# Linear attention in chunks of 128 tokens for all heads at once, in front of two MLPs, on one Trainium2 core

## The chip, the cores and the metric

One Trainium2 chip, one of its cores. The metric is device microseconds (us) of one execution; lower is better. The engines are named as in the profile: PE (TensorE, with its weight loads as PEld), DVE (VectorE), ACT (ScalarE), POOL (GpSimd) and SP (SyncE, which issues most DMAs).

## The reference

Batch 4, 8 heads, 768 tokens, head width 48. A linear attention with a decay per channel, and two MLPs over the 3072 tokens:

```
for t in range(S):
    state = alpha[:, :, t, :, None] * state + np.einsum('bhd,bhe->bhde', k[:, :, t], v[:, :, t])
    y[:, :, t] = np.einsum('bhd,bhde->bhe', q[:, :, t], state)
x = y, heads side by side            # 3072 x 384
h = x @ w_in                         # 384 -> 2048
x = (h * sigmoid(h)) @ w_out         # 2048 -> 384
h = x @ w2_in                        # 384 -> 1024
solu = h * softmax(h)
ln = (solu - mean) / sqrt(var + 1e-06) * g_ln
out = ln @ w2_out                    # 1024 -> 384
```

## The kernel before

The tokens are cut into nine units: three of 256 tokens (batch 0) and six of 384. Attention works by chunks of 128 tokens: running products of alpha are taken with scans on DVE, q is multiplied by the product and k divided by it, and then within a chunk it is a masked product of scores with v, and between chunks a state of 48 x 48 for each head. Two heads form a pair: one on partitions 0 to 47, the other on 64 to 111.

Before, a step of attention is one pair over all the chunks of a unit (class Pair, 36 of them, four for each unit): one load `x` of q, k and alpha, two scans (`scan`, `back`), `rec`, `qmul`, `mul`; on PE the transposes of k (`tr`, line 566), the scores (`scores`, line 587), the state's contribution (`state`, lines 607 and 608), the masked scores by v (`outs`, line 638) and q by the carried state (line 645). `masked` copies one head's scores by a predicated copy on DVE, the other's by ACT and POOL. `carry` brings the state on, chunk by chunk, with tiny operations. `evac` (ACT) and `rest` (DVE) split the result into two fp32r parts in `y_all`; the fourth pair goes to `yt` and from there by DMA (`holes`) into the rows that the other three leave free, so the first MLP sees 3 x 128 full rows.

The first MLP runs in blocks: a block is 128 of the 2048 hidden features for one unit, six groups of three matmuls (three groups into `h`, lines 769 to 771; three into `x`, lines 804 to 806, two blocks later). Its weights come as packed words in 16 pieces (`d` load, `r`, `z`, `u`, `y` unpack, `c` and `p` split into two parts); a piece holds the columns or rows of two blocks. VISITS says in which order units go through the blocks.

The program has a fixed order for each engine. For the first 270 groups it is the string ORDER, one letter for a step (`a` scores, `o` outs, `p` last step of a weight piece, `g3` three groups of the MLP, and so on); a star picks another engine. After that each unit's attention is spread evenly over the MLP blocks of the unit before it (`unit_steps`). The second MLP follows for all tokens; attention is over by then.

Of the kernel before, what the change touches and what calls it, by code (L numbers as in the profile page):

```python
# [7 lines left out]
U8 = mybir.dt.uint8  # L8
# [12 lines left out]
HP = 112  # L21
KC, KF, KB = DM // 128, DFF // 128, DF2 // 128
# [4 lines left out]
RB, FB = 4, 3  # L27
# [10 lines left out]
x0 w0 K0 n0 x1 w1 i0 R0 x2 m0* q0* n1 t0 a0 F3 k0 w2 B0 x3 v0 R1 n2 d0 f0 d1 w3 d2 i1 i2 A0 R2 s0 d3* q1* r0 S0 m1  # L38
q2* t1 R3 o0 a1 k1* n3 i3 K1 f2 f1 r1 e0 B1 A1 z0 s1 m2 q3 m3 z1 t2 a2 S1* x4 o1 k2* s2 B2 A2 E0 u0 y0 e1 u1* x5 c0
S2 w4 v1 a3 d4 y1 t3 E1 r2 o2 e2 B3 k3 s3 h3 c1 p0* x6 f3 z2 A3* E2 w5 S3* o3 r3 p1 h2 r4 h1 e3 g1 u2 y2 g1 z3 u3*  # L40
z4 n4 F6 y3 E3 c2 p2* u4* c3 g1 x7 g1 p3* q4 y4 d5 r5 c4 d6 z5 d7 r6 g1 L0 g1 i4 u5 d8 R4 y5 g1 L1 g1 z6 m4 u6* f4
t4 a4 y6 p4* w6 c5 k4 g1 A4 r7 s4 p5* g2 B4 n5 R5 g1 i5 S4* L2* z7 g1 r8 m5 g1 z8 u7* o4 e4 g1 w7 c6 g1 x8 g1 d9* v2
g1 t5 q5* E4 R6 n6 p6* k5 g1 a5 A5 g1 y7 d10 f5 w8 i6 g1 R7 B5* s5 S5* L3* L4 m6 g2 c7 g3 n7 o5 e5 p7* g2 f6 t6 q6
i7 k6 E5 L5* g1 a6 m7 A6 B6 d11* f7 x9 s6 u8 S6 g1 o6 e6 y8 E6 t7 g1 q7 k7 g1 a7 B7* s7 c8 A7 h5 S7 g1 r9 o7 g1 e7
r10 E7 g1 h6 p8 z9 g1 L6 g1 r11 g1 d12* g3 u9 z10 h7 L7* u10* x10 g1 y9 g2 z11 g1 u11* g5 y10 g1 y11 d13 g1 c9 g2
c10 g2 L8 g1 p9* L9* p10* r12 z12 g1 x11 g1 u12* g1 L10* g1 d14 g2 y12 g2 L11 n8 g2 c11 g1 r13 p11* g1 c12 r14 g1
z13 d15 g1 p12* g2 L12 g1 z14 u13* g2 r15 g1 q8* g2 y13 g2 u14* L13* R8 i8 L14 c13 g6 y14 c14 m8 w9 w10 g1 z15 L15
u15* y15 g4 f8 g6 t8 p14* L16* k8* g2 n9 a8 c15 g1 i9 g4 s8 A8* g1 R9 g3 B8* m9 g1 L17* S8* g1 w11 p13* o8 t9 g1 n10
k9 L19 g1 s9 g2 R10 g1 L18 n11 g1 i10 g1 e8 g1 f9 g1 E8 g1 q9 S9* g3 m10 g1 a9 g2 L20 p15* g3 A9* B9* L21* R11 g3
L22* g2 o9 g2 e9 g1 q10 g2 L23* g1 t10 g1 E9 g1 i11 g1 m11 a10 k10 h9 s10 B10* g1 A10 S10 L24* g1 f10 g2 o10 e10 g2  # L50
t11 g3 L25 g2 E10 k11* q11 g2 s11 a11 g1 A11 S11 h10 B11* g3 o11 L26 g2 e11 E11 g2 L27 h11 g5 f11 g2 L28 W0 g1 x12
g2 L29* g3 w12 v3 x13 L30 g2 x14 n12 g3 q12* i12 g4 L31 g3 R12 g4 m12 g3 x15 w13 g1 v4 n13 L33 t12 L32 R13 k12 g1
a12 s12 g3 S12* g1 w14 q13* g3 i13 g1 A12 g1 L34* n14 g4 B12* m13 g1 o12 w15 t13 f12 L35* L36 g3 i14 g2 k13* R14 f13
g1 e12 g1 m14 q14* g1 E12 s13 L37 g4 a13 B13 A13* n15 L38* i15 x16 S13* g7 o13 g3 L39 w16 g1 n16 e13 g3 E13 a14 g1
R15 x17 g1 t14 w17 g1 B14 A14* g1 i16 g1 L40 g2 m15 k14* g1 q15* g4 s14 g2 L41* S14* o14 e14 t15 g2 R16 k15 E14 g3
f15 L42 a15 s15 m16 S15 f16 A15* B15 h14* g1 f14 g6 o15 L43* q16 g1 e15 g2 E15 g2 h15 x18 h13*
"""
RANGE = 1e28
LEAST = 1e-14
# [6 lines left out]
PAIRS = (3, 0, 1, 2)  # L66
VISITS = [(0, 0, 8), (1, 0, 8), (0, 8, 16), (1, 8, 16)] + [(u, 0, 16) for u in range(2, NU)]
# [104 lines left out]
def general(tc, qka, vt, w_in, w_out, w2_in, w2_out, g_ln, ident, mhalf, out):  # L172

    nc = tc.nc
    with (
# [4 lines left out]
        with (  # L180
# [8 lines left out]
            for p in range(H // 2):  # L189
                with tc.For_i(0, B, 1) as b:  # L190
                    x = ga.tile([HP, 3, S], F32, name="x")
                    nc.sync.dma_start(out=x, in_=qka[bass.ds(b, 1), p].rearrange("o p k s -> (o p) k s"))
# [53 lines left out]
        with (  # L246
# [4 lines left out]
            with tc.For_i(0, NT, 128) as t0:  # L251
                xt = p.tile([128, KC, 128], F32, name="xt")
                for kc in range(KC):
                    for r0, n, h0 in (
                        (0, 48, 96 * kc), (48, 16, 288 + 32 * kc), (64, 48, 96 * kc + 48), (112, 16, 304 + 32 * kc)
                    ):
                        nc.sync.dma_start(out=xt[r0 : r0 + n, kc, :], in_=yT[h0 : h0 + n, bass.ds(t0, 128)])
# [44 lines left out]
def body(tc, qka, v, vt, w_in, w_out, w2_in, w2_out, g_ln, out):  # L302
    nc = tc.nc
    with tc.tile_pool(name="const", bufs=1) as const, tc.tile_pool(name="dram", bufs=1, space=DRAM) as dram:
        ident = const.tile([128, 128], F32, name="ident")
        mask = const.tile([128, CH], I8, name="mask")
        flags = const.tile([HP, 2, NU * 4], F32, name="flags")
# [5 lines left out]
        main(tc, const, ident, mask, flags, ones, mhalf, good, x2d,  # L313
             qka, v, w_in, w_out, w2_in, w2_out, g_ln, out)

        cnt = nc.values_load(good[0:1, 0:1], min_val=0, max_val=HP)
# [4 lines left out]
def main(tc, const, ident, mask, flags, ones, mhalf, good, x2d,  # L321
# [12 lines left out]
    width = W0  # L334
    stage, att = push("stage1"), push("att0")
# [12 lines left out]
    spare = psa.tile([128, 512], F32, tag="sc", name="spare")  # L348
# [7 lines left out]
    NJ = NU * 4  # L356
    x_t, xe_t, ar_t, rb_t, ra_t = {}, {}, {}, {}, {}
    v_t, y_t, st_t, yt_t = {}, {}, {}, {}

    def upj(j):  # L360
        return j // 4, PAIRS[j % 4]

    def load_x(j, queue=nc.sync):
        if j >= NJ or j in x_t or UNITS[j // 4][2] != width:
            return
        u, p = upj(j)
        b, t0, n = UNITS[u]
        xe_t[j] = att.tile([HP, 3 * width + 1], F32, tag="x", bufs=4, name="x")
        x = xe_t[j][:, : 3 * width].rearrange("p (k s) -> p k s", k=3)
        for sl in (slice(2, 3), slice(0, 2)) if j == 0 else (slice(0, 3),):  # L370
            queue.dma_start(out=x[:, sl, :n], in_=qka[b, p, :, sl, t0 : t0 + n])
        x_t[j] = x

    def load_v(u):
        if u >= NU or UNITS[u][2] != width:
            return
        b, t0, n = UNITS[u]
        t = att.tile([128, width // CH, DM], F32, tag="v", bufs=2, name="v")
        nc.sync.dma_start(out=t[:, : n // CH, :], in_=v[b, t0 : t0 + n, :].rearrange("(c s) e -> s c e", s=CH))
        v_t[u] = t  # L380

    least = const.tile([128, 1], F32, name="least")
    nc.gpsimd.memset(least, -LEAST)
# [3 lines left out]
    d1, dr, ms = [], [], []  # L387

    def persistent():

        d1[:] = [att.tile([HP, width], F32, name=f"d1{i}") for i in range(2)]
        ms[:] = [[att.tile([128, width // CH, CH], F32, name=f"ms{i}{h}") for h in range(2)] for i in range(2)]
        dr[:] = [att.tile([HP, width], F32, name="dr")]
        for i in range(2):
            nc.gpsimd.memset(d1[i], FLOOR)
            if i == 0:
                nc.gpsimd.memset(dr[0], 0.0)
                nc.gpsimd.memset(dr[0][:, ::CH], 1.0)
            for h in range(2):
                nc.gpsimd.memset(ms[i][h], 0.0)  # L400

    persistent()
# [756 lines left out]
```

## Time and profile before

| | |
|---|---|
| median of 3 runs | 785.31 us (784.7 to 788.0) |
| the profiled execution | 786.08 us, of which 784.4 us from the first to the last instruction (the span) |
| PE, DVE, ACT, POOL busy | 96%, 54%, 46%, 19% of the span |
| instructions | 13575, of which 5290 on PE |
| mean granted PE clock | 0.993 of full speed |

Matmuls are pipelined: one is shown as busy for longer than the time after which the next can start. What a matmul costs is read from the distance between the starts of matmuls, not from its duration. An fp32 matmul of the attention stands as two instructions in the trace, an fp32r matmul of the MLPs as one.

### The profile page before, as it was taken

The page shows a single profiled execution, that of the slowest core. Times are in us where ns is not written, and L with a number is a line of the kernel's source. Part 1 is how long each engine was busy: PE and PEld are TensorE (multiplying, and loading weights), DVE is VectorE, ACT ScalarE, POOL GpSimd, SP SyncE. Part 2 cuts the span into 40 slices and gives each one's busy share as a digit, 9 for nine tenths or more (in the row PEclk, how much of TensorE's full clock was granted, in tenths as well). Part 3 has the DMA queues.
Part 4 walks back from the last instruction along what each step waited for, and adds up shares of the span by engine and source line. Part 5 has one row for each costly group of instructions (what it writes and reads, how often), then busy time and mean ns, then how long its engine had stood idle before and what let it go on. Part 6 is the DMA issues. An engine that isn't in the chain of part 4 may idle for free.

```text
span 784.4 us, 13575 instructions
## 1 busy us (share of the span) xinstructions
PE 756.9 (96%) x5290; PEld 693.8 (88%) x5291; DVE 421.6 (54%) x906; ACT 359.1 (46%) x838; POOL 150.5 (19%) x261
## 2 busy tenths in 40 slices
PE   5688999999999999999999999999999999999996
PEld 3467999999999999999999999999889999999996
DVE  6897953755443543533452442269555555555552
ACT  4766933444333433433333333377444444444442
POOL 5224413222111201211111210000221121112110
PEclk9989999999999999999999999999999999999999
DMA  8836103514122113112211100073111111111001
GB/s 268 282 123 211 55 5 96 146 32 116 34 57 62 58 38 89 57 32 76 76 33 32 62 6 6 7 272 101 61 51 41 41 41 41 47 45 50 31 21 36
DMA packets 35657, 57.59 MB, mean 73 GB/s; under 512 B 3040, under 2 KB 30496, under 8 KB 35584
## 3 DMA queue, kind: packets, MB, share of 16 engines
q1 hardware_dynamic: 34880, 53.30, 21.9%
q10 hardware_dynamic: 704, 3.34, 1.2%
q8 instruction: 43, 0.70, 0.4%
q14 instruction: 30, 0.25, 0.1%
HBM read 44.83 MB, written 9.44 MB: 69 GB/s over the span
## 4 chain that ended last, share of the span: by engine, by line
PE 90%; DMA 1%; ACT 1%; POOL 1%; DVE 1%; issue 0%; SPq 0%; POOLq 0%; ACTq 0%
PE x L804 9%; PE h L769 9%; PE x L805 8%; PE x L806 8%; PE h L770 8%; PE h L771 8%; PE h L1020 4%; PE o L1068 4%; PE h L1021 4%; PE h L1022 4%; PE o L1066 4%; PE o L1067 4%; PE sc L587 3%; PE y L638 3%; PE tp L1045 3%; PE y L645 3%
## 5 line engine op out<-in xcount | busy, mean ns | idle before, releaser
L775 ACT ACTIVATE g<-h 128x384 fp32r<-128x384 f32 (+1 forms) x144 | 65.8, 457 | 196.8 <-PE h L771 196.4
L769 PE MATMUL h<-y_all,w1i 128*128 128x384 f32 (+1 forms) x432 | 144.2, 334 | 4.9 <-DMA y_all<-yt 4.9
L804 PE MATMUL x<-g,w1o 128*128 128x384 f32 (+1 forms) x432 | 143.0, 331 | 0.0
L805 PE MATMUL x<-g,w1o 128*128 128x384 f32 (+1 forms) x432 | 138.3, 320 | 1.3 <-POOL g L779 1.3
L770 PE MATMUL h<-y_all,w1i 128*128 128x384 f32 (+1 forms) x432 | 138.4, 320 | 0.0
L771 PE MATMUL h<-y_all,w1i 128*128 128x384 f32 (+1 forms) x432 | 138.3, 320 | 0.0
L806 PE MATMUL x<-g,w1o 128*128 128x384 f32 (+1 forms) x432 | 138.1, 320 | 0.0
L769 PEld LDWEIGHTS h<-y_all,w1i 128*128 128x128 f32 x432 | 82.8, 192 | 10.4 <-issue 8.4
L779 DVE TENSOR_TENSOR g<-g,g 128x384 fp32r<-128x384 f32 (+1 forms) x125 | 67.8, 545 | 39.3 <-ACT g L776 39.2
L804 PEld LDWEIGHTS x<-g,w1o 128*128 128x128 f32 x432 | 82.4, 191 | 4.9 <-issue 2.8
L805 PEld LDWEIGHTS x<-g,w1o 128*128 128x128 f32 x432 | 82.5, 191 | 1.7 <-POOL g L779 1.7
L770 PEld LDWEIGHTS h<-y_all,w1i 128*128 128x128 f32 x432 | 83.0, 192 | 0.1
L771 PEld LDWEIGHTS h<-y_all,w1i 128*128 128x128 f32 x432 | 82.9, 192 | 0.0
L806 PEld LDWEIGHTS x<-g,w1o 128*128 128x128 f32 x432 | 82.4, 191 | 0.0
L596 POOL TENSOR_SCALAR_AFFINE_SELECT ms<-ms 128x384 f32<-128x384 f32 (+1 forms) x39 | 22.4, 579 | 267.4 <-ACT ms L595 267.3
L1066 PE MATMUL o<-w2o,ct 128*128 128x384 f32 x192 | 66.5, 346 | 0.0
L776 ACT ACTIVATE g<-h 128x384 f32<-128x384 f32 (+1 forms) x144 | 65.2, 453 | 0.7 <-POOL g L779 0.7
L1068 PE MATMUL o<-w2o,ct 128*128 128x384 f32 x192 | 64.7, 337 | 0.0
L1067 PE MATMUL o<-w2o,ct 128*128 128x384 f32 x192 | 64.6, 337 | 0.0
L666 DVE TENSOR_TENSOR y_all<-y,y_all 112x384 fp32r<-112x384 f32 (+2 forms) x28 | 14.2, 508 | 91.2 <-ACT y_all L661 91.1
L132 DVE TENSOR_REDUCE nm<-h 128x1 f32<-128x1024 f32 x24 | 29.4, 1224 | 57.7 <-PE h L1022 57.7
L1020 PE MATMUL h<-w2i,x 128*128 128x512 f32 x144 | 56.8, 394 | 0.0
(121 smaller groups left out, 1356.3 us busy)
## 6 DMA issues: line engine op xcount, KB each, us to landing
x<-in_qka_dram SPq DMA_DIRECT2D x24, 504.0 KB, 4.4
raw<-in_w_in_dram SPq DMA_DIRECT2D x10, 768.0 KB, 6.9
raw<-in_w_out_dram SPq DMA_DIRECT2D x8, 768.0 KB, 6.2
x2f<-x2d SPq DMA_DIRECT2D x24, 192.0 KB, 2.8
out_dram<-ob SPq DMA_DIRECT2D x24, 192.0 KB, 1.9
x<-in_qka_dram SPq DMA_DIRECT2D x11, 336.0 KB, 4.8
v<-in_v_dram SPq DMA_DIRECT2D x6, 576.0 KB, 5.3
x2d<-x_all SPq DMA_DIRECT2D x5, 576.0 KB, 2.7
```

Of the source, the lines that this page charges most:

```text
L769: nc.tensor.matmul(h, w1i[:, 0, kc, fs], Y[:, kc, 0, :n], start=(kc == 0), stop=False)
L770: nc.tensor.matmul(h, w1i[:, 0, kc, fs], Y[:, kc, 1, :n], start=False, stop=False)
L771: nc.tensor.matmul(h, w1i[:, 1, kc, fs], Y[:, kc, 0, :n], start=False, stop=(kc == KC - 1))
L775: nc.scalar.activation(out=g[:, 0, :n], in_=h, func=AF.Silu)
L779: eng.tensor_tensor(out=g[:, 1, :n], in0=g32[:, :n], in1=g[:, 0, :n].bitcast(F32), op=ALU.subtract)
L804: nc.tensor.matmul(x, w1o[:, 0, f, msl], g[:, 0, :n], start=first, stop=False)
L805: nc.tensor.matmul(x, w1o[:, 0, f, msl], g[:, 1, :n], start=False, stop=False)
L806: nc.tensor.matmul(x, w1o[:, 1, f, msl], g[:, 0, :n], start=False, stop=last)
L1020: nc.tensor.matmul(h[:, sl], x[:, 0, kc, :], self.w2i[:, 0, kc, sl], start=(kc == 0), stop=False)
L1066: nc.tensor.matmul(o, ct[:, 0, kb, :], self.w2o[:, 0, kb, :], start=(kb == 0), stop=False)
L1067: nc.tensor.matmul(o, ct[:, 0, kb, :], self.w2o[:, 1, kb, :], start=False, stop=False)
L1068: nc.tensor.matmul(o, ct[:, 1, kb, :], self.w2o[:, 0, kb, :], start=False, stop=(kb == KB - 1))
```

## The change

A step of attention is now one chunk of 128 tokens with all four pairs side by side (class Chunk, 24 of them, two or three for each unit). The same scans, products, transposes, scores and sums are made, four pairs of 128 columns in one instruction on DVE, ACT and POOL where there were two or three chunks of one pair. The products of k and q take their input from a layout in which a chunk is contiguous; the reciprocal of a chunk's last product now goes into the start of the backward scan, so that `mul` is one plain product; the two flags of a pair become one. `carry` is one or two operations for all heads. Both masked copies run on DVE in `unit_steps`; the ORDER string chooses for the first units.

In `outs` the even pairs go to PSUM bank sA and the odd ones to sB, and an odd pair's heads are swapped: head 0 on input partitions 0 to 47 is written to output partitions 64 to 111, and head 1 the other way round. The scores use the same two banks. The fourth pair's rows are again moved by `holes`, now all six DMAs at the end of a unit. Rows of `w_in` are permuted to fit.

Pools: three buffers instead of four for loaded `x` and for raw weights, one d1 tile instead of two. VISITS gives the first two units blocks 0 to 4 and 0 to 8, then 4 to 16 and 8 to 16. ORDER is written anew; it holds no filling matmuls (`F`). At the end the last store is issued by ACT, and the flag of the check is read into the engines' registers ahead of it.

```diff
-RB, FB = 4, 3
+XB, RB, FB = 3, 3, 3
...
-VISITS = [(0, 0, 8), (1, 0, 8), (0, 8, 16), (1, 8, 16)] + [(u, 0, 16) for u in range(2, NU)]
+VISITS = [(0, 0, 4), (1, 0, 8), (0, 4, 16), (1, 8, 16)] + [(u, 0, 16) for u in range(2, NU)]
...
+            nc.vector.tensor_tensor_scan(
+                out=rb_t[c][:, ::-1], data0=xe_t[c][:, o + NS : o : -1], data1=dr, initial=0.0,
+                op0=ALU.mult, op1=ALU.max,
+            )
...
+        def mul(eng=nc.vector):
+            x = x_t[c]
+            eng.tensor_tensor(out=x[:, 1, :], in0=x[:, 1, :], in1=rb_t[c], op=ALU.mult)
...
+            for p in range(NP):
+                sl = slice(p * CH, p * CH + CH)
+                for i, (lo, hi) in enumerate(HD):
+                    nc.tensor.matmul(self.sc[i][:, p, :], x[lo:hi, 1, sl], x[lo:hi, 0, sl], start=True, stop=True)
...
+            if not self.first:
+                nc.vector.tensor_tensor(out=st[:, 1], in0=z, in1=st_t[self.c - 1][:, 0], op=ALU.add)
+                z = st[:, 1]
+            nc.vector.tensor_tensor(out=st[:, 0], in0=z, in1=ends, op=ALU.mult)
...
+            self.y = y = [self.bank(t, o) for t, o in (("sA", "x1"), ("sB", "x2"))]
+            where = []
+            for p in range(NP):
+                sl = slice(p // 2 * CH, p // 2 * CH + CH)
+                for i, (lo, hi) in enumerate(HD):
+                    where.append((p, i, lo, hi, y[p % 2], 64 * (i ^ (p % 2)), sl))
+            for p, i, lo, hi, bank, r, sl in where:
+                w = D if r else 64
+                e0 = (2 * p + i) * D
+                nc.tensor.matmul(
+                    bank[r : r + w, sl], vv[:, e0 : e0 + w], ms[i][:, p, :],
+                    start=p < 2, stop=self.first, skip_group_check=True,
+                )
+            if not self.first:
+                st = st_t[self.c - 1]
+                for p, i, lo, hi, bank, r, sl in where:
                     nc.tensor.matmul(
+                        bank[r : r + D, sl], st[lo:hi, 0, p, :], x[lo:hi, 0, p * CH : p * CH + CH],
+                        start=False, stop=True, skip_group_check=True,
                     )
...
             r += [
+                step(0, [lambda c=c: load_x(c + XB - 1), lambda c=c: load_v(c + 1), Q.tr, Q.keep]),
+                step(1, [Q.scores, lambda Q=Q: Q.masked(0, True), lambda Q=Q: Q.masked(1)]),
+                step(2, [Q.state, Q.outs, lambda Q=Q: Q.evac(1), lambda Q=Q: Q.evac(0), Q.carry]),
+                step(3, [lambda Q=Q: Q.rest(1), lambda Q=Q: Q.rest(0)]),
             ]
+        return r + [lambda: [holes(u, kc) for kc in range(KC)]]
...
+            if i == n - 1:
+                queue = nc.scalar
+                self.cnt = nc.values_load(self.good[0:1, 0:1], min_val=0, max_val=HP)
+            queue.dma_start(out=self.out[t : t + 128, :], in_=ob)
```

PE, one visit of `outs` from the fourth unit on. Before, one pair over three chunks, the two heads in turn (ms is the masked scores, v the values, x holds q, st the carried state; the size is partitions by columns of the output):

```order
L638 MATMUL y<-ms_1598,v 64x128
L638 MATMUL y<-ms_1599,v 48x128
L638 MATMUL y<-ms_1598,v 64x128
L638 MATMUL y<-ms_1599,v 48x128
L638 MATMUL y<-ms_1598,v 64x128
L638 MATMUL y<-ms_1599,v 48x128
L645 MATMUL y<-x,st 48x128 x4
```

And now, one chunk with four pairs:

```order
L608 MATMUL sA<-ms_108,v 64x128
L608 MATMUL sA<-ms_109,v 48x128
L608 MATMUL sB<-ms_108,v 48x128
L608 MATMUL sB<-ms_109,v 64x128
L608 MATMUL sA<-ms_108,v 64x128
L608 MATMUL sA<-ms_109,v 48x128
L608 MATMUL sB<-ms_108,v 48x128
L608 MATMUL sB<-ms_109,v 64x128
L615 MATMUL sA<-x,st 48x128 x2
L615 MATMUL sB<-x,st 48x128 x2
L615 MATMUL sA<-x,st 48x128 x2
L615 MATMUL sB<-x,st 48x128 x2
```

A unit of 384 tokens now has three such visits where it had four; each holds four pairs. Output partitions run 0, 64, 64, 0 in the L608 rows where they ran 0, 64, 0, 64, and pairs of rows alternate between two banks.

DVE, around the last weight piece (the last `p`, line 458 before, line 450 now; `g` is the low part of an MLP block, `f` a weight piece being unpacked). Before:

```order
L482 SCALAR_TENSOR_TENSOR ar<-x,d_107 112x256
L500 RECIPROCAL ra<-ar 112x2
L666 TENSOR_TENSOR yt<-y,yt 112x256
L623 TENSOR_TENSOR st<-tz,st 112x48
L509 SCALAR_TENSOR_TENSOR x<-x,ra,rb 112x128 x2
L779 TENSOR_TENSOR g<-g_1253,g 128x256
L458 TENSOR_TENSOR w1o<-f,w1o 128x768
```

Now:

```order
L642 TENSOR_TENSOR yt<-sB,yt 112x128
L642 TENSOR_TENSOR y_all<-sB,y_all 112x128
L642 TENSOR_TENSOR y_all<-sA,y_all 112x2x128
L91 SCALAR_TENSOR_TENSOR f<-f 128x768
L100 TENSOR_SCALAR f<-f 128x768
L744 TENSOR_TENSOR g<-g_1157,g 128x256
L106 SCALAR_TENSOR_TENSOR f<-raw,f 128x768
L744 TENSOR_TENSOR g<-g_1213,g 128x256
L450 TENSOR_TENSOR w1o<-f,w1o 128x768
```

Ahead of the last piece there stood the first result of the third unit (its `yt`, the first of its four pairs); now all six chunks of the first three units are finished there. In the order of the whole program, 127 groups of the MLP stood ahead of the last `p` before, and 136 stand there now.

## Rows read from the trace of the kernel before

**Rows 1.** The page: busy us, share of the span, instructions by engine.

```profile
PE 756.9 (96%) x5290; PEld 693.8 (88%) x5291; DVE 421.6 (54%) x906; ACT 359.1 (46%) x838; POOL 150.5 (19%) x261
```

**Rows 2.** Timeline, PE, the start (start us, us, idle and its releaser in brackets).

```profile
30.66 0.55 PE L769 MATMUL h<-y_all,w1i 128*128 128x256 f32 x1 [3.19 <-DMA y_all<-yt]
...
37.03 0.28 PE L770 MATMUL h<-y_all,w1i 128*128 128x256 f32 x1
37.15 0.28 PE L771 MATMUL h<-y_all,w1i 128*128 128x256 f32 x1
41.82 0.58 PE L566 MATMUL tz<-ident,x 112*128 112x112 f32 x2 [4.39 <-DVE x L509]
```

**Rows 3.** Windows up to the last weight piece: all engines, then lines 769, 804, 638.

```profile
0.00:107.00 107.00, 86.05 (x670) 72.11 (x672) 86.52 (x164) 71.29 (x174) 39.23 (x75) 0.95 0.52 172
...
0.00:107.00 107.00, 21.27 (x66) 13.82 (x66) 0.95 0.52 172
...
0.00:107.00 107.00, 18.14 (x58) 12.01 (x59) 0.95 0.52 172
...
0.00:107.00 107.00, 8.57 (x72) 5.51 (x72) 0.95 0.52 172
```

**Rows 4.** Groups by line and shape, DVE, whole span (busy us, mean ns).

```profile
L482 DVE TENSOR_TENSOR_SCAN ar<-x,d 112x384 f32<-112x384 f32 x24 | 24.4, 1015 | 1.3 <-DMA v<-in_v_dram 1.3
L593 DVE COPY_PREDICATED ms<-mask,sc 128x384 f32<-128x384 uint8 x24 | 14.2, 592 | 35.2 <-PE sc L587 35.2
L482 DVE TENSOR_TENSOR_SCAN ar<-x,d 112x256 f32<-112x256 f32 x12 | 9.1, 758 | 5.0 <-POOL x L470 5.0
L593 DVE COPY_PREDICATED ms<-mask,sc 128x256 f32<-128x256 uint8 x9 | 3.8, 439 | 4.0 <-PE sc L587 4.0
```

**Rows 5.** Timeline, DVE: the last weight piece.

```profile
106.96 0.95 DVE L458 TENSOR_TENSOR w1o<-f,w1o 128x768 fp32r<-128x768 f32 x1
```

**Rows 6.** Timeline, PE, 200 to 220 us: attention's visits among the MLP's matmuls.

```profile
206.61 0.34 PE L806 MATMUL x<-g,w1o 128*128 128x384 f32 x1
206.79 0.36 PE L566 MATMUL tz<-ident,x 112*128 112x112 f32 x2
...
207.17 0.34 PE L805 MATMUL x<-g,w1o 128*128 128x384 f32 x1
...
209.43 0.34 PE L771 MATMUL h<-y_all,w1i 128*128 128x384 f32 x1
209.70 0.26 PE L607 MATMUL tz<-v,kt 128*64 128x48 f32 x1
...
209.92 0.88 PE L638 MATMUL y<-ms,v 128*48 128x128 f32 x12
210.73 0.86 PE L645 MATMUL y<-x,st 48*48 48x128 f32 x12
...
211.80 0.34 PE L805 MATMUL x<-g,w1o 128*128 128x384 f32 x1
211.98 0.34 PE L806 MATMUL x<-g,w1o 128*128 128x384 f32 x1
...
214.58 0.34 PE L771 MATMUL h<-y_all,w1i 128*128 128x384 f32 x1
214.85 0.94 PE L587 MATMUL sc<-x 48*128 48x128 f32 x12
...
216.00 0.34 PE L805 MATMUL x<-g,w1o 128*128 128x384 f32 x1
```

**Rows 7.** Timeline, PE: the same line earlier, with eight instructions.

```profile
56.09 0.65 PE L638 MATMUL y<-ms,v 128*64 128x128 f32 x8
```

**Rows 8.** Timeline, PE's weight loads and matmuls of one visit.

```profile
236.99 0.63 PEld L638 LDWEIGHTS y<-ms,v 128*64 128x64 f32 x12 [0.25 <-issue]
236.99 0.87 PE L638 MATMUL y<-ms,v 128*64 128x128 f32 x12
```

**Rows 9.** The page: DMA issues, KB each, us to landing.

```profile
raw<-in_w_in_dram SPq DMA_DIRECT2D x10, 768.0 KB, 6.9
```

More of the change, by code (lines that the diff above doesn't have):

```diff
@@ L532, in prep_pieces, with prepare @@
+        if c <= LEDC:
             return dict(n=scan, q=qmul, R=back, i=rec, m=mul, f=flag)
-        return [first, back, rec, mul, flag]
-    queue = [(j, f) for j in range(4 * LED + 1, NJ) for f in prep_pieces(j)]
-    def prepare(j, part=1.0):
-        if j not in x_t:
+        return [first, second, mul, flag]
+    queue = [(c, f) for c in range(LEDC + 1, NC) for f in prep_pieces(c)]
+    def prepare(c, part=1.0):
+        if c not in x_t:
             return
-        left = sum(1 for jj, _ in queue if jj <= j)
+        left = sum(1 for cc, _ in queue if cc <= c)
@@ L601, in state @@
         def state(self):
-            kt, tz, vv, p = self.kt, self.tz, v_t[self.u], self.p
-            z = tz[:HP, 3 * HP : 3 * HP + 3 * D].rearrange("p (c e) -> p c e", e=D)
-            h0 = 2 * p * D
-            for c in range(self.nz):
-                k0 = c * HP
-                nc.tensor.matmul(z[0:64, c, :], kt[:, k0 : k0 + 64], vv[:, c, h0 : h0 + D], start=True, stop=True)
+            if self.last:
+                return
+            kt, vv = self.kt, v_t[self.c]
+            self.z = z = self.tz[:HP, : NP * D].rearrange("p (c e) -> p c e", e=D)
@@ new lines, in evac, with rest, holes @@
+        def evac(self, k):
+            for y, hi, _ in self.places(k):
+                nc.scalar.copy(hi, y)
+        def rest(self, k):
+            for y, hi, lo in self.places(k):
+                nc.vector.tensor_tensor(out=lo, in0=y, in1=hi.bitcast(F32), op=ALU.subtract)
+    def holes(u, kc, queue=nc.sync):
+        n = UNITS[u][2]
+        for r in range(2):
+            j = 32 * kc + 16 * r
+            src = j if j < D else 64 + j - D
+            queue.dma_start(
+                out=y_t[u][48 + 64 * r : 64 + 64 * r, kc, :, :n].bitcast(F32),
+                in_=yt_t[u][src : src + 16, :, :n].bitcast(F32),
+            )
@@ L687, in unit_steps, with step @@
     def unit_steps(u):
         r = []
-        pairs = [Pair(j) for j in range(4 * u, 4 * u + 4)]
-        def close(P):
-            return [P.outs, P.evac, P.rest] + ([P.holes] if P.p < 3 else [])
-        for k, P in enumerate(pairs):
-            j = P.j
-            def step(i, fns, j=j):
+        for c in range(NC):
+            if UNIT_OF[c] != u:
+                continue
+            Q = Chunk(c)
+            def step(i, fns, c=c):
                 def run():
                     if i == 0:
-                        prepare(j)
+                        prepare(c)
@@ L744, in step @@
         if letter in "xvw":
-            return dict(x=lambda j: load_x(j, queue), v=load_v, w=floors)[letter](i)
-        if letter in "FKW":
-            return dict(F=lambda: fill(i), K=halves if i else constants, W=widen)[letter]()
-        P = first[i]
+            return dict(x=lambda c: load_x(c, queue), v=load_v, w=floors)[letter](i)
+        if letter in "FK":
+            return dict(F=lambda: fill(i), K=halves if i else constants)[letter]()
+        if letter == "h":
+            return holes(i // KC, i % KC, queue)
+        Q = first[i]
         return dict(
-            t=P.tr, k=lambda: P.keep(other), a=P.scores, A=lambda: P.masked(0, other),
-            B=lambda: P.masked(1, other), s=P.state, S=lambda: P.carry(other),
-            o=P.outs, e=P.evac, E=P.rest, h=lambda: P.holes(queue),
+            t=Q.tr, k=lambda: Q.keep(other), a=Q.scores, A=lambda: Q.masked(0, other),
+            B=lambda: Q.masked(1, other), s=Q.state, S=Q.carry, o=Q.outs,
+            e=lambda: Q.evac(0), E=lambda: Q.rest(0), j=lambda: Q.evac(1), J=lambda: Q.rest(1),
         )[letter]()
@@ L808, in fn @@
                     xs = xs_of(u)
-                    if blocks[gi][1] >= KF // 2 and (u, 0, KF) not in VISITS:
+                    if again[gi]:
                         nc.vector.tensor_tensor(out=xs[:, m, :], in0=x, in1=xs[:, m, :], op=ALU.add)
@@ L822, in main @@
     visits = VISITS
-    blocks = []
+    blocks, again = [], []
     start = {}
```

389 lines of the change are left out of this document (150 added, 239 removed).

## The prediction

> **What bounds the kernel now.** I read the page first: PE is busy for 96% of the span and no other engine for more than 54% [rows 1], so what counts is PE's own work, and the places where PE has none. The timeline of PE at the start is next: the first MLP matmul begins at 30.66 us, and after 37.15 us PE stops for 4.39 us behind DVE [rows 2]. The windows tell why: up to the last weight piece, which DVE starts at 106.96 us [rows 5], DVE is busy for 86.5 of 107 us, ACT for 71.3, and the clock averages 0.95 [rows 3]. So there are two stretches. To about 108 us DVE sets the pace: it unpacks weights and prepares attention while PE waits or fills in. Behind that PE sets it. The second is read from the timeline in the middle, where MLP matmuls of 384 columns start 0.17 to 0.18 us apart and attention visits stand between them [rows 6]. What a visit costs is the time from the last matmul ahead of it to the second behind it, less two matmuls (0.35 us), since that second one is the first to run at its usual distance.
>
> **The change part by part, behind 108 us.** The counts of matmuls stay: 192 scores, 192 masked products, 160 with the state, 160 state sums, 80 transposes. What changes is how many share a visit. From [rows 6]: 12 score instructions 216.00 - 214.58 - 0.35 = 1.07 us; two transposes 207.17 - 206.61 - 0.35 = 0.21; a visit of 8 state, 12 masked and 12 carried instructions 211.80 - 209.43 - 0.35 = 2.02. Four more instructions of 128 columns cost 0.22 (x12 takes 0.87 or 0.88, x8 takes 0.65 [rows 6, 7]), so two run at a time at 0.11 a pair. Eight state instructions take 209.92 - 209.70 = 0.22.
>
> Before, units 3 to 8 (three batches of two units): a pair of a batch's first unit has 12 state, 12 masked and 8 carried instructions and three transposes, 0.32 + 1.07 + (2.02 + 0.11 - 0.22) = 3.30 us; one of its second unit 0.21 + 1.07 + 2.02 = 3.30. Eight pairs make 26.4 us a batch. After, a chunk has 16 of each: scores 1.07 + 0.22 = 1.29; four transposes 0.42 (between 0.21, if it is all overhead, and twice that; I take the upper); a full outs visit 2.02 + 0.22 + 0.22 + 0.22 = 2.68. The first chunk of a batch has nothing carried (12 instructions, 0.66, less): 2.02 + 0.22 + 0.22 - 0.66 = 1.80; the last has no state sums and no transposes: 2.02 - 0.22 + 0.44 = 2.24. A batch: 6 x 1.29 + 5 x 0.42 + 4 x 2.68 + 1.80 + 2.24 = 24.6 us. That is 1.8 less, **5.4 us** for three batches, from entering and leaving the visits' array modes three times a unit instead of four. Below zero it cannot go, since no instruction is added.
>
> The swap comes on top. Before, the carried products alternate between two 64 x 64 quarters of the array (input rows 0 to 47 to output 0 to 47, and 64 to 111 to 64 to 111), and 12 of them take six times 0.11. Now an even and an odd pair together use all four quarters, with the odd pair in another bank. No row shows four quarters at work. Bounds: 0.88 us for 16 if still two run at a time, 0.44 if four do. I take four: the state visit shows that instructions can start every 0.22 / 8 = 0.028 us [rows 6], and four in 0.11 need just that. Five chunks a batch carry: 5 x 0.44 = 2.2, **6.6 us** for three batches.
>
> Here the Trainium skill speaks against it. [rows 8] show weight loads for the next masked products going on (0.63 us, all 12) inside the 0.87 us of matmuls that use the same 128 input rows. TensorE: Matmul & The Clock Gate (Part 3, "What overlaps and what doesn't") says that a weight load overlaps matmuls in flight only when the row group differs; TensorEngine Tiling (Restrictions and Gotchas, Gotcha 1) that different row tiles cannot be in one PSUM bank at once. By the first, two quarters on the same input rows would take turns and the 6.6 us would not come; the trace does not bear it out for two column halves. By the second, the old pair of quarters, which shares bank y, would take turns too, and 0.11 us for two shows that it does not.
>
> The masked products now go to outputs 0, 64, 64, 0. Each half gets as many as before; I cost the order at nothing (at most half again of 0.88 us: 0.44 for each of 24 chunks, 10 us).
>
> DVE behind 108 us: a chunk asks for about 6.5 us, three in a unit's 61 us, so only bursts matter. The longest is two masked copies (592 ns at 384 columns and 439 at 256 [rows 4], so 0.745 at 512), the reciprocal (0.2) and a backward scan (1.15): 2.8 us, and then the 0.56 us for the low part of a block. That part is needed 18 matmuls of 0.17 us (3.1 us) behind where it is queued; a burst that hits it squarely costs 0.3 us. With the six DMAs of holes now all at a unit's end I allow **1 us** in all (0 to 4).
>
> **Up to 108 us.** Priced by row means, with 512 columns carried on from 256 and 384 (scan 758, 1015, so 1272 ns [rows 4]), DVE's list up to its last weight piece sums to 96.4 us before and 95.5 after: weights 47.5 and 45.1, MLP low parts and copies 6.7 and 8.1, attention 42.2 and 42.3. So I leave the last piece at 107.9 us. What differs is what PE has done by then. Before: (66 + 58) instructions of lines 769 and 804 are 124 groups, and 72 / 8 = nine pairs have their y [rows 3]; a tenth has its scores and transposes. After, 136 groups and all six chunks, which are twelve pairs, stand ahead of that piece in the order. Twelve groups of three matmuls 0.12 apart [rows 2] are 4.3 us; three pairs of 256 tokens at 0.85 + 0.21 + (2.02 - 0.44) = 2.64 are 7.9, less 1.05 for the tenth's start: **11.2 us**. PE can have done it: from 30.66 us, 136 x 0.36 = 49 and four chunks of 4.4 = 18 lead to 97 us, ten under the piece. Bounds: DVE idles for 20 of the 107 us, and half of that may go with the fewer small steps (21 us gained); six more us of waits for the second unit leave 5.
>
> The store by ACT and the early flag: I take nothing.
>
> **The sum**, against the profiled execution: 784.4 - 11.2 - 5.4 - 6.6 + 1.0 = 762.2 us of span; that execution took 1.7 us more than its span, so **763.9 us**. It was 786.1, 0.8 above the median.
>
> **The rivals.** *Two quarters at a time*: the 6.6 us stay away, 770.5. *Nothing won at the start*: the second unit's MLP blocks are due after four blocks of the first instead of eight. If its two chunks are late (four DVE-bound chunks at some 6 us of DVE work each, with three pieces between), PE idles there, the clock falls, and the 11.2 us are given back: 775.1. For it: PE already waited for DVE in that place. Against: DVE's list has these chunks at 42 us of its own work. *Slower: the raw weights' ring.* Three buffers instead of four. Before, 16 pieces in about 103 us are 25.7 us a turn of a buffer, of which the load takes 6.9 [rows 9] and four unpacking steps at 0.95 another 3.8; the rest is waiting. If a turn keeps its 25.7 us, three buffers need 137 us, the last piece lands some 33 us late and the time is about 797 (763.9 + 33). It decides from a turn of about 24 us on, where the whole gain is gone. Against: the waiting is for DVE and ACT, which the new order serves piece by piece. *No change*: two at a time and nothing won at the start, 781.7.
>
> **How the numbers follow.** Forecast as summed 0.42, two at a time 0.24, nothing won at the start 0.18 (some of it with two at a time), no change 0.08, slower 0.08. The range 750 to 777 runs from the sum with 10 us more at the start and some cover for the 1 us, to nothing won at the start with 2 us more of bursts. Changes within 0.5% (3.9 us) can't be told from none here: faster 0.86, same 0.07, slower 0.07.
>
> **What would show it.** Line 615 x16 in 0.6 us (four quarters) or about 1.0 (two); an outs visit among 384-column matmuls at 2.2 or 2.7 us; scores at 1.3; the last piece of line 450 at 100 to 108 us, with some 136 instructions of lines 734 and 769 and 96 of line 608 ahead of it; no idle in front of PE's lines 735 and 770 behind 110 us. I am wrong if PE waits for line 450 or for `y_all` for over 10 us past 45 us, if masked products take over 1.3 us for 16, or if bursts on DVE stop PE each chunk.

## The result, and the profile after

The changed kernel takes 762.98 us (median of 4 runs, 761.04 to 764.04), the kernel before 785.98 beside it (784.7 to 788.0): a ratio of 0.970, with a 95% interval from 0.967 to 0.973. The profiled execution took 764.04 us, with a span of 762.3: 22.0 us less than the span of before. The forecast was 763.9.

The page of the changed kernel, busy time by engine, beside [rows 1]:

```profile
PE 726.5 (95%) x5282; PEld 682.2 (89%) x5282; DVE 404.4 (53%) x728; ACT 342.0 (45%) x730; POOL 138.4 (18%) x196
```

PE has eight instructions fewer; DVE has 178 fewer and is busy for 17 us less. PE is still the bound.

Timeline of PE in the changed kernel: the start with five of its six longest gaps, block 8 (the ninth block), and the only gap of over 1 us from 60 to 108 us, beside [rows 2]:

```profile
12.41 0.58 PE L557 MATMUL sA<-x 48*128 48x128 f32 x1 [12.41 <-DVE x L485]
...
20.82 0.58 PE L557 MATMUL sA<-x 48*128 48x128 f32 x1 [1.95 <-DVE x L485]
...
33.82 0.58 PE L557 MATMUL sA<-x 48*128 48x128 f32 x1 [4.16 <-POOL x L485]
...
36.52 0.56 PE L734 MATMUL h<-y_all,w1i 128*128 128x256 f32 x1
...
54.91 0.34 PE L557 MATMUL sA<-x 48*128 48x128 f32 x1 [4.68 <-DVE x L485]
...
59.23 0.55 PE L734 MATMUL h<-y_all,w1i 128*128 128x256 f32 x1 [1.68 <-DMA y_all<-yt]
...
69.24 0.28 PE L734 MATMUL h<-y_all,w1i 128*128 128x256 f32 x1
...
91.72 0.39 PE L770 MATMUL x<-g,w1o 128*128 128x256 f32 x1 [1.59 <-DVE g L744]
```

The first MLP matmul comes six us later than before (36.52 against 30.66), yet PE has caught up by block 8 (69.24 us; before, 70.37). Windows of the changed kernel (busy us and instructions of PE, PEld, DVE, ACT, POOL, then granted clock, DMA share, GB/s): all engines to 107 us, lines 734, 769 and 608 alone, beside [rows 3], then two stretches:

```profile
0.00:107.00 107.00, 77.96 (x753) 72.11 (x754) 86.75 (x127) 68.66 (x137) 34.43 (x50) 0.97 0.61 186
...
0.00:107.00 107.00, 20.22 (x67) 13.74 (x68) 0.97 0.61 186
...
0.00:107.00 107.00, 17.61 (x60) 11.75 (x60) 0.97 0.61 186
...
0.00:107.00 107.00, 8.79 (x96) 7.11 (x96) 0.97 0.61 186
...
31.00:61.00 30.00, 20.66 (x218) 18.58 (x219) 29.44 (x45) 18.16 (x36) 8.35 (x11) 0.91 0.72 216
...
75.00:108.00 33.00, 31.41 (x314) 29.98 (x313) 29.20 (x43) 24.62 (x54) 11.07 (x8) 1.00 0.39 130
```

All six chunks have their masked products (96) by 107 us, but only 67 + 60 = 127 MLP instructions of these two lines stand beside them, three more than before. From 75 to 108 us PE lacks 1.59 us, and that is the one wait at 91.72. The last weight piece, beside [rows 5], is three and a half us later than before:

```profile
110.47 0.96 DVE L450 TENSOR_TENSOR w1o<-f,w1o 128x768 fp32r<-128x768 f32 x1 [0.57 <-ACT w1o L447]
```

The visits are as forecast. Timeline of PE in the changed kernel, a full visit for the outputs, beside [rows 6] (the fp32 instructions stand one by one here):

```profile
256.25 0.34 PE L736 MATMUL h<-y_all,w1i 128*128 128x384 f32 x1
256.52 0.26 PE L579 MATMUL sT<-v,kt 128*64 128x48 f32 x1
...
257.16 0.47 PE L608 MATMUL sB<-ms,v 128*48 128x128 f32 x4
257.38 0.47 PE L608 MATMUL sA<-ms,v 128*48 128x128 f32 x4
257.60 0.47 PE L608 MATMUL sB<-ms,v 128*48 128x128 f32 x4
258.00 0.31 PE L615 MATMUL sA<-x,st 48*48 48x128 f32 x2
258.01 0.31 PE L615 MATMUL sB<-x,st 48*48 48x128 f32 x2
258.15 0.28 PE L615 MATMUL sA<-x,st 48*48 48x128 f32 x2
258.16 0.28 PE L615 MATMUL sB<-x,st 48*48 48x128 f32 x2
258.26 0.28 PE L615 MATMUL sA<-x,st 48*48 48x128 f32 x2
258.27 0.28 PE L615 MATMUL sB<-x,st 48*48 48x128 f32 x2
...
258.59 0.45 PE L769 MATMUL x<-g,w1o 128*128 128x384 f32 x1
258.87 0.34 PE L770 MATMUL x<-g,w1o 128*128 128x384 f32 x1
```

By the measure of the prediction the visit costs 258.87 - 256.25 - 0.35 = 2.27 us (2.24 forecast with four quarters, 2.68 with two). Line 615 starts four instructions every 0.11 us; the masked products, all on 128 input rows, two (four every 0.22). Over the stretch from 190 to 470 us the medians are 1.30 for scores, 0.40 for transposes, 2.27, and 1.68 and 1.81 for the first and last chunk: 6 x 1.30 + 5 x 0.40 + 4 x 2.27 + 1.68 + 1.81 = 22.4 us a batch, and the forecast was 24.6 - 2.2 = 22.4.

### The profile page after: what moved, and what is told of

It is laid out like the page before. It is cut to its first block, busy times and chain, and to the rows that moved or that the text cites. A ratio compares the mean times of both kernels' runs of the same rounds, so it can differ in the third digit from the quotient of the medians.

```text
span 762.3 us, 13151 instructions
## 1 busy us (share of the span) xinstructions
PE 726.5 (95%) x5282; PEld 682.2 (89%) x5282; DVE 404.4 (53%) x728; ACT 342.0 (45%) x730; POOL 138.4 (18%) x196
## 4 chain that ended last, share of the span: by engine, by line
PE 91%; DMA 3%; DVE 3%; ACT 2%; issue 1%; SPq 0%; DVEq 0%; ACTq 0%
PE h L734 9%; PE x L769 9%; PE x L770 9%; PE x L771 9%; PE h L736 9%; PE h L735 8%; PE o L1030 4%; PE h L984 4%; PE o L1031 4%; PE h L985 4%; PE h L986 4%; PE o L1032 4%; PE sA L557 3%; PE tp L1009 3%; DMA raw<-in_w_out_dram 2%; PE sA L608 1%
## 5 line engine op out<-in xcount | busy, mean ns | idle before, releaser
L740 ACT ACTIVATE g<-h 128x384 fp32r<-128x384 f32 (+1 forms) x144 | 65.9, 458 | 165.7 <-PE h L736 165.6
L769 PE MATMUL x<-g,w1o 128*128 128x384 f32 (+1 forms) x432 | 139.0, 322 | 0.0
L770 PE MATMUL x<-g,w1o 128*128 128x384 f32 (+1 forms) x432 | 137.3, 318 | 1.6 <-DVE g L744 1.6
L771 PE MATMUL x<-g,w1o 128*128 128x384 f32 (+1 forms) x432 | 137.2, 317 | 0.0
L744 DVE TENSOR_TENSOR g<-g,g 128x384 fp32r<-128x384 f32 (+1 forms) x126 | 71.2, 572 | 85.3 <-ACT g L741 84.8
L984 PE MATMUL h<-w2i,x 128*128 128x512 f32 x144 | 57.0, 396 | 0.0
L985 PE MATMUL h<-w2i,x 128*128 128x512 f32 x144 | 56.9, 395 | 0.0
L986 PE MATMUL h<-w2i,x 128*128 128x512 f32 x144 | 56.9, 395 | 0.0
```

Source lines behind the costliest of these rows:

```text
L769: nc.tensor.matmul(x, w1o[:, 0, f, msl], g[:, 0, :n], start=first, stop=False)
L770: nc.tensor.matmul(x, w1o[:, 0, f, msl], g[:, 1, :n], start=False, stop=False)
L771: nc.tensor.matmul(x, w1o[:, 1, f, msl], g[:, 0, :n], start=False, stop=last)
L984: nc.tensor.matmul(h[:, sl], x[:, 0, kc, :], self.w2i[:, 0, kc, sl], start=(kc == 0), stop=False)
L985: nc.tensor.matmul(h[:, sl], x[:, 0, kc, :], self.w2i[:, 1, kc, sl], start=False, stop=False)
L986: nc.tensor.matmul(h[:, sl], x[:, 1, kc, :], self.w2i[:, 0, kc, sl], start=False, stop=(kc == KC - 1))
```

## The experiments

Each was timed with the kernel before on the same chip. The interval is that of the ratio; the span is that of the profiled execution. Block 8 is the start of the ninth block's first MLP matmul in the profile (69.2 us in the changed kernel).

| kernel | median us (lowest to highest) | ratio [95%] | span | block 8 |
|---|---|---|---|---|
| no swap | 769.25 (766.5 to 770.98) | 0.978 [0.975, 0.982] | 768.6 | 69.0 |
| state apart | 769.32 (767.25 to 769.77) | 0.979 [0.977, 0.982] | 765.5 | 68.5 |
| m2 on DVE | 762.91 (761.21 to 763.65) | 0.971 [0.968, 0.973] | 761.3 | 68.6 |
| two chunks first | 762.24 (761.05 to 766.3) | 0.972 [0.968, 0.975] | 759.3 | 66.4 |
| three signs left out | 761.02 (760.47 to 763.48) | 0.968 [0.965, 0.971] | 759.0 | 65.9 |
| transposes with scores | 763.78 (762.54 to 765.39) | 0.971 [0.968, 0.973] | 762.9 | 69.9 |
| last store by SP | 763.13 (one run) | | 761.4 | 68.8 |
| two chunks first, store by SP | 761.74 (760.09 to 764.39) | 0.970 [0.969, 0.972] | 762.6 | 69.6 |
| the same, two signs elsewhere | 762.61 (761.17 to 764.69) | 0.972 [0.970, 0.974] | 761.1 | 68.4 |
| the same, two low parts elsewhere | 762.53 (761.77 to 762.97) | 0.972 [0.970, 0.973] | 760.8 | 67.9 |
| the changed kernel again | 763.27 (762.43 to 764.53) | 0.973 [0.972, 0.974] | 762.2 | 69.2 |
| fifteen signs left out | 760.89 (758.56 to 761.72) | 0.968 [0.965, 0.970] | 760.0 | 69.1 |

**Is it the four quarters?** The swap alone is taken back, with the row maps that belong to it.

```diff
-    swap = kc % 2
+    swap = 0
...
-                    where.append((p, i, lo, hi, y[p % 2], 64 * (i ^ (p % 2)), sl))
+                    where.append((p, i, lo, hi, y[p % 2], 64 * i, sl))
```

> The changed kernel with the odd pairs not swapped: head 0 of every pair goes to output partitions 0 to 47, head 1 to 64 to 111, in the same two banks, and the rows of the first weight matrix are permuted to fit; all else stays. Theory (the swap lets four quarters of the array work at once): the 16 carried products of a chunk take 0.87 us in place of about 0.44, an outs visit 2.7 us in place of 2.27, and with 20 such chunks, 13 of them behind block 48, the time is 6 to 9 us more than the changed kernel's 763, so 769 to 772. Rival (the products gained by sharing a visit, and the quarters take turns anyway): no change, 763. Second rival (the order 0, 64, 64, 0 of the masked products holds them up): some of the loss is given back in line 608, and the time is below 769.

The carried products of one visit in its timeline of PE:

```profile
260.26 0.42 PE L615 MATMUL sA<-x,st 48*48 48x128 f32 x4
260.51 0.39 PE L615 MATMUL sB<-x,st 48*48 48x128 f32 x4
260.73 0.39 PE L615 MATMUL sA<-x,st 48*48 48x128 f32 x4
260.95 0.39 PE L615 MATMUL sB<-x,st 48*48 48x128 f32 x4
```

Now four take 0.22 us, two at a time. All other visits keep their price, and the full one costs 2.70 instead of 2.27: 0.42 more, where 0.44 was reckoned. From unit 3's first block to the last matmul of the first MLP 13 visits make 5.5, and that stretch is 5.3 us longer (365.9 against 360.6); the time rose by 6.3. So the swap is worth what the forecast said, and two banks without it are worth nothing. Whether the swap within one bank would do as much was not tried.

**Is a visit's entry what the rest of the gain is?** The state sums go into a visit of their own.

```diff
-                step(2, [Q.state, Q.outs, lambda Q=Q: Q.evac(1), lambda Q=Q: Q.evac(0), Q.carry]),
+                Q.state,
+                step(2, [Q.outs, lambda Q=Q: Q.evac(1), lambda Q=Q: Q.evac(0), Q.carry]),
```

> The changed kernel with the state sums of a chunk in a step of their own from the fifth unit on, so that each of 12 chunks there has four visits of PE in place of three; no instruction is added. Theory (entering and leaving a visit costs PE time, which is what four pairs in a visit save): each apart visit costs 0.33 us, the difference in the trace of before between the two apart (0.68 + 1.57) and the two together (1.92); 12 x 0.33 = 4 us, 767. Rival (visits cost nothing, the gain came from the swap and the start alone): 763.

The end of a state visit in its timeline of PE (line 735 is the MLP's):

```profile
256.16 0.28 PE L579 MATMUL sT<-v,kt 128*64 128x48 f32 x2
256.37 0.44 PE L735 MATMUL h<-y_all,w1i 128*128 128x384 f32 x1
256.65 0.34 PE L736 MATMUL h<-y_all,w1i 128*128 128x384 f32 x1
```

The two visits cost 0.79 + 1.81 us against 2.27 together: 0.33 more, as forecast, and 12 of them 3.9. The same stretch is 4.2 us longer. The median rose by 6.3, more than that; the profiled execution, at 767.25, was its shortest, so the other 2 us are in no profile and stay open.

**Does every visit have this price?** The opposite: the transposes join the scores' visit.

```diff
-                step(0, [lambda c=c: load_x(c + XB - 1), lambda c=c: load_v(c + 1), Q.tr, Q.keep]),
-                step(1, [Q.scores, lambda Q=Q: Q.masked(0, True), lambda Q=Q: Q.masked(1)]),
+                step(0, [lambda c=c: load_x(c + XB - 1), lambda c=c: load_v(c + 1)]),
+                step(1, [Q.tr, Q.scores, Q.keep, lambda Q=Q: Q.masked(0, True), lambda Q=Q: Q.masked(1)]),
```

> The changed kernel with the four transposes of a chunk in the visit of its scores instead of a visit of their own; only the chunks of units 4 to 8, 12 with transposes. If every visit costs a fixed price of about 0.35 to 0.4 us for entering and leaving, as the prediction reckoned it for three visits instead of four, 12 fewer give 4.2 to 4.8 us: 758 to 759 us, and the merged visit takes 1.30 + 0.05. If the price is that of going over to quarters of the array, which the scores pay anyway, and transposes on all rows pay only the 0.09 us by which the second matmul behind them is late, 12 give 1.1 us: 762, and the merged visit takes 1.6 us.

```profile
250.99 0.34 PE L736 MATMUL h<-y_all,w1i 128*128 128x384 f32 x1
251.17 0.55 PE L538 MATMUL sT<-ident,x 112*128 112x112 f32 x4
251.64 0.37 PE L557 MATMUL sA<-x 48*128 48x128 f32 x1
...
252.74 0.45 PE L734 MATMUL h<-y_all,w1i 128*128 128x384 f32 x1
253.02 0.34 PE L735 MATMUL h<-y_all,w1i 128*128 128x384 f32 x1
```

This is the merged visit in its timeline of PE: 253.02 - 250.99 - 0.35 = 1.68 us, against 0.40 + 1.30 apart. Nothing is won (0.02 a chunk), and both theories were too high. Behind an MLP matmul the transposes start at its usual distance of 0.18, so entering costs them nothing. What is saved, 0.09 at leaving them and 0.10 at the scores' own entry, comes back between the two: the scores begin 0.47 us behind the transposes, where in the changed kernel the MLP begins 0.32 behind. This fits a price for going over to parts of the array, and not one for each visit; these two regroupings are all that was tried.

**Does DVE's list pace the start?** First, the long product of chunk 2, in front of which PE stands for 4.16 us, is moved from POOL to DVE (`m2*` becomes `m2` in ORDER).

> The changed kernel with the product of k of the third chunk on DVE in place of POOL, for whose result PE waits 4.2 us just ahead of the first MLP block. Theory (in the first 60 us DVE's list sets when the second unit is ready, and PE's waits there only change their place): the first MLP block starts 1 to 4 us earlier, PE waits as much longer ahead of the fourth block, and the time is within 1 us of 763. Rival (each wait of PE at the start counts in full): 759.

No change, and block 8 at 68.6: PE's wait ahead of these scores stays where it was (4.99 us at 32.79), now for DVE. Then the order of DVE's list: the first two chunks' scans and products stand ahead of the first weight piece.

```diff
-x0 w0 d0 v0 K1 r0 n0 x1 x2* i0 R0 v1 q0* z0 d1 m0 u0* K0 y0 a0 t0 w1 n1 f0 B0 w2 i1 k0 s0 r1 A0* o0 q1* d2 c0 r2 j0
+x0 w0 x1 d0 v0 K1 n0 v1 x2 d1 i0 R0 q0* m0 K0 a0 t0 w1 n1 i1 q1* R1 A0* m1 r0 z0 u0* y0 f0 B0 w2 k0 s0 r1 o0 d2 c0 r2 j0
```

> The changed kernel with another order of the first 30 us alone: the load of the second chunk goes ahead of the first weight piece, and the preparation of both chunks stands on DVE ahead of the first unpacking step, which there waits 3.1 us for its load with the product of the first chunk behind it. Theory (the start lost time because attention's first chain stood behind a weight load; PE has no idle time behind 61 us, so what the start loses is lost for good): the first scores at 8 to 9 us in place of 12.4, the first MLP block 3 to 6 us earlier than 36.5, and the time 2 to 5 us less, 758 to 761. Rival (weights are what the start waits for): the first MLP block comes earlier, the following ones do not, and the time is the same or longer.

Its profile was 3.0 us shorter, its median only 0.7, well within the spread of its runs. Then work is left out: the step that gives the sign back to the weights.

```diff
-... q0* z0 d1 m0 ... t1 z1 d3 f1 ... c2 z3 n3 f2 ...
+... q0* d1 m0 ... t1 d3 f1 ... c2 n3 f2 ...
```

> The changed kernel without the step that gives the sign back (line 91 on DVE) to weight pieces 0, 1 and 3, so these weights are wrong; the other pieces keep it. That takes three DVE instructions of about 0.95 us from the first 55 us, 2.9 us in all. If DVE's list sets the pace there, the first MLP matmul of block 4 comes 2 to 3 us earlier than 59.2 us, that of block 8 2 to 3 us earlier than 69.2, and the run ends at 760 to 761 us. If transfers set the pace (the DMA engines are 82% busy up to 31 us), block 4 moves by less than 1 us and the time stays at 763.

This looked like proof: block 8 at 65.9, 3.3 us earlier, and 761.02. But "two chunks first" had looked as good in one profile, so it was run again with the store, beside two ways to take 1.9 us from DVE without leaving anything out (`z1`, `z3` starred; `p2`, `p3` unstarred) and the changed kernel itself.

> The changed kernel with two edits that looked better in a trace alone: the preparation of the first two chunks ahead of the first weight piece (the span was 3.0 us shorter with it), and the last store on SP's queue (0.46 us shorter tail). If both are real, they add: 763.0 - 2.6 (block 8 came at 66.4 instead of about 69.0 us) - 0.5 = 759.9 us. Rival: a start that is earlier in one profile is within what the start varies by from run to run (block 8 came at 68.5 to 69.9 us in six kernels that start alike), and the median stays at 762 to 763.

> The kernel with both edits, and the signs of weight pieces 1 and 3 given back by ACT and POOL (0.9 us and 2.1 us) instead of DVE (0.95 us). If what counts at the start is the sum of DVE's list, as the run without three signs says (3.1 us earlier for 2.9 us less), block 8 comes 1.9 us earlier than in the kernel with both edits: at 64.5 us, and the time falls by 1.9 us. Rival: the piece is late by the longer way over two engines, and DVE waits for it in its next step of the same piece: no gain, or a loss of 1 to 2 us.

> The kernel with both edits, and the low parts of weight pieces 2 and 3 on POOL (2.4 us each) instead of DVE (0.95 us). Nothing on DVE waits for a low part, only the matmuls of blocks 2 and 3. If the sum of DVE's list counts, block 8 comes 1.9 us earlier, at 64.5 us. Rival: POOL's other work behind it, the products of line 485 and the half of the masked copies, comes 2.4 us later and holds up the scores: no gain or a loss.

> The changed kernel once more, beside the three others on one chip: 763 us, with block 8 at 68.5 to 69.9 us. If the three others gain what was said, it stands 3 to 5 us behind them.

The 66.4 us of block 8 did not come back: the same start gave 69.6, and with 1.9 us less on DVE 68.4 and 67.9, not 64.5. On this chip all four medians lie within 1.6 us, with intervals that overlap; none is a faster kernel that could be vouched for. The last run takes the sign from fifteen of the sixteen pieces.

> The changed kernel without the step that gives the sign back (line 91 on DVE) to fifteen of the sixteen weight pieces of the first MLP, so these weights are wrong. It takes seven DVE instructions (6.5 us) from the first 61 us and eight more behind them. If DVE's list paces the first 61 us, block 8 comes 5 to 6.5 us earlier than the 68.5 to 69.9 us of the kernels that start alike, at 62.5 to 64 us, and since PE is busy without a break from about 61 us on, the eight later ones give nothing more: 757 to 758 us. If DVE paced PE up to 108 us, as the prediction said, all fifteen would count: 749 us. Rival: transfers or the steps on ACT and POOL pace the start, what the run without three signs gained was the spread of the starts, and the time stays at 761 to 763.

The theory falls: some 14 us of DVE's work are gone, and 2 us were won. The start of block 8 in its timeline of PE, and windows of this kernel, the same two stretches as above:

```profile
69.15 0.28 PE L734 MATMUL h<-y_all,w1i 128*128 128x256 f32 x1
```

```profile
31.00:61.00 30.00, 22.17 (x221) 20.04 (x222) 24.74 (x40) 18.08 (x36) 8.76 (x10) 0.74 0.76 221
75.00:108.00 33.00, 33.00 (x329) 31.76 (x328) 24.32 (x40) 25.83 (x56) 7.41 (x8) 1.00 0.46 142
```

DVE has 4.7 us less to do between 31 and 61 us, and block 8 comes at 69.1 all the same. (PE, granted 0.74 of its clock there instead of 0.91, is busy for 1.5 us more, so that much of a gain may be hidden; 5 to 6.5 us were expected.) The 2 us that were won lie behind: block 16 starts at 88.7 us (88.8 with the signs), block 20 at 98.6 (100.5), because the one wait at 91.72 is gone and PE is busy for 33.00 of 33. Why three signs left out gave more at block 8 than fifteen is open. In that profile the second weight piece landed earliest of all (below), but only 0.75 us ahead of the next, which is too little for 3 us.

What holds the first MLP matmul is seen on the queues. ACT in the changed kernel, then DVE (timelines):

```profile
9.88 0.89 ACT L85 ACTIVATE f<-raw 128x768 f32<-128x768 f32 x1 [7.57 <-DMA raw<-in_w_in_dram]
...
17.55 0.91 ACT L85 ACTIVATE f<-raw 128x768 f32<-128x768 f32 x1 [1.55 <-DMA raw<-in_w_out_dram]
18.35 0.82 ACT L447 CAST w1i<-f 128x768 fp32r<-128x768 f32 x1
```

```profile
19.20 0.96 DVE L450 TENSOR_TENSOR w1i<-f,w1i 128x768 fp32r<-128x768 f32 x1 [1.28 <-ACT w1i L447]
20.08 0.68 DVE L485 TENSOR_TENSOR x<-x,ar 112x512 f32<-112x512 f32 x1
```

The second chunk's product (line 485 at 20.08) stands behind the low part of piece 0, this waits for the cast of piece 0, and the cast stands behind the first step of piece 1, which waits for its load. In all nine profiles that begin in this order, two with signs left out among them, that load ends between 15.0 and 19.6 us; the second chunk's scores start 3.3 us later and the first MLP matmul 18.2 to 19.7 us later. The transfer sets this chain, and DVE is one link. That casting piece 0 ahead of piece 1's first step would free it was not tried.

A second transfer stands ahead of block 4, the wait at 59.23. From the chain of work that ended last, in the changed kernel and then with fifteen signs left out:

```profile
52.52 6.57 DMA y_all<-yt
```

```profile
51.73 6.79 DMA y_all<-yt
```

These are two of the six DMAs of `holes` for the second unit. In the changed kernel they land 5.7 to 6.8 us after their issue, where those of the first unit took 2.0 to 2.2. The load of an `x`, issued 1.3 us ahead of them, lands at 57.92, and the first of them at 58.45. In the kernel with two low parts elsewhere that load landed as they were issued; they took 2.0 to 2.3 us, and PE did not wait for them. So part of the wait is where the transfers stand. With fifteen signs left out DVE finishes this unit 0.8 us earlier (51.05 against 51.85 us), and block 4 starts 0.6 us earlier. Another order of these transfers was not tried, and what else paces the stretch stays open.

**The last store.** SP instead of ACT, in one run.

```diff
-                queue = nc.scalar
+                queue = nc.sync
```

> The changed kernel with its last store back on the queue of SP; the flag is still read ahead of it. Theory: the store lands in 3.1 us as before instead of 4.1, and from the start of the last activation to the end it takes 6.0 to 6.4 us instead of 6.66. Rival: the 0.3 us more come from reading the flag ahead of the store, and stay.

From the last activation to the end it takes 6.20 us (755.20 to 761.40) against 6.66 with ACT (755.65 to 762.31); the kernel before took 6.37. One run cannot tell them apart: the nine profiles with the store by ACT took 6.19 to 6.66 us, the four changed kernels with SP 6.20 to 6.57. Neither a price of ACT's queue nor a gain by the early flag is shown.

## Why the forecast was right, and where it was not

The total is right within 1 us, and part of that is luck: errors that cancel. The first row is worked out from what PE had done by 107 us in each kernel, at the forecast's prices; the second is the rest of the 23.2 us that the traces show up to the last matmul of the first MLP.

| stretch | forecast us | measured us |
|---|---|---|
| up to 107 us | -11.2 | -8.0 |
| from there to the last matmul of the first MLP | -5.4 - 6.6 + 1.0 = -11.0 | -15.2 |
| behind it | 0 | +1.1 |
| span | -22.2 | -22.0 |

**Up to 107 us** the term was mis-sized: of 12 more groups three came, 1.1 us instead of 4.3; the three pairs (7.9, less 1.05) did come. The step behind it, "To about 108 us DVE sets the pace", failed in the main. DVE is as busy as forecast (86.75 of 107 us, and 29.44 of 30 from 31 to 61 us), but from 61 us on PE lacks nothing up to 108 except at 91.72, and in front of 61 us seven instructions less on DVE (6.5 us) moved block 8 by 0.1 us in one profile; with eight more gone behind them, the time fell by 2 us of 14. So the last piece's place (110.47, not 100 to 108) decided nothing either.

**The visits** came out as summed, with both parts shown by a run: 0.42 us a visit for the four quarters (0.44 reckoned), and 0.33 for one visit with state sums split into two. The first rule of the Trainium skill that was weighed against the 6.6 us did not hold here: by TensorE: Matmul & The Clock Gate (Part 3, "What overlaps and what doesn't"), as the prediction read it, quarters on the same input rows would take turns, and four instructions start in 0.11 us. The masked order 0, 64, 64, 0 costs nothing, as taken: four in 0.22, as before.

**Behind 107 us** 4.2 us more came than forecast. The kernel before was dearer than the one visit of [rows 6] says: seven times behind 107 us its state sums stood in a visit of their own (0.684 + 1.571 us against 1.922 together), 0.33 each, some 2.3 in all. The 1.0 us for bursts on DVE was not needed: PE waits for nothing behind 110 us up to the end of the first MLP. The burst was put together wrongly, too: in `unit_steps` only one of the two masked copies runs on DVE (line 562), the other on ACT and POOL (lines 566 and 567), not both on DVE as the sections ahead of the prediction say. The backward scan behind it takes 1.64 us there, not 1.15 (last section). And an MLP matmul follows the last after 173.1 ns instead of 173.4 (mean behind block 48, visits apart), 0.6 us over 1745. These make 3.9 of the 4.2.

**The end** was costed at nothing and lost 1.1 us: 0.3 behind the last activation, which is within the spread of the profiles, and 0.8 in the second MLP, whose tiles take 9.28 instead of 9.24 us. No run told why.

**The rivals.** Two quarters at a time would have been 770.5; the run without the swap has it, at 769.25. The ring of three raw buffers did not bind as feared: the last piece came 3.5 us later, not 33, and the loads land in 4.4 to 4.6 us where [rows 9] had 6.9. Nothing won at the start, and no change, fall with the table above.

## What to carry to other kernels

Price a group of small matmuls by what it shares with its neighbours: splitting one visit on parts of the array into two cost 0.33 us here, joining whole-array transposes to scores on parts of it won 0.02, and the four quarters of the array, over two banks, ran four instructions at once. An engine that is busy for 98% of a stretch need not pace it alone: take some of its work away and see whether the next milestone moves, before its list is priced. And a start that is 3 us earlier in one profile may be the spread of the start; run it again.

## What the runs showed of the hardware that was not expected

A backward scan (line 474, 512 columns) takes 1.21 to 1.27 us in the start of the changed kernel, but 2.87 when an addition on POOL lies over it. Timelines of POOL and of DVE, with two other pairs:

```profile
25.22 1.41 POOL L567 TENSOR_SCALAR_AFFINE_SELECT ms<-ms 128x512 f32<-128x512 f32 x1 [3.33 <-ACT ms L566]
...
29.20 2.15 POOL L95 TENSOR_TENSOR f<-f,raw 128x768 f32<-128x768 f32 x1 [1.50 <-ACT raw L94]
...
175.09 0.64 POOL L567 TENSOR_SCALAR_AFFINE_SELECT ms<-ms 128x512 f32<-128x512 f32 x1 [1.60 <-ACT ms L566]
```

```profile
24.99 1.20 DVE L465 TENSOR_TENSOR_SCAN ar<-x,d 112x512 f32<-112x512 f32 x1
...
29.55 2.87 DVE L474 TENSOR_TENSOR_SCAN ar<-x,dr 112x512 f32<-112x512 f32 x1
...
175.17 1.63 DVE L474 TENSOR_TENSOR_SCAN ar<-x,dr 112x512 f32<-112x512 f32 x1
```

The addition and the scan overlap for 1.80 us and the scan loses 1.6. The Trainium skill (GPSIMD Engine Reference, 8. Key points) names such a contention for DVE instructions with two inputs in SBUF; here it costs nearly the whole overlap. In these rows who loses goes by who began. The low part at 28.69 had begun before the addition and takes its usual 0.95 us. From 175 us on, fourteen backward scans begin just behind POOL's part of a masked copy and take 1.63 to 1.64 us. At 24.99 the scan had begun first and keeps its 1.20 us, and POOL's part takes 1.41 instead of 0.64. One pair does not fit: at 95.66 a scan begins under a POOL operation on 112 x 4 elements (line 455) and takes its usual 1.21 us.
